# Spectral filter, soft MoE and GLU on one core: filters loaded by units instead of by channel halves, and the second step's first stage moved into a block

## The chip, the cores and the metric

The kernel runs on one core of a Trainium2 chip. The metric is the time of one execution in microseconds of device time; the median of three executions is taken.

## The reference

```python
# x (8, 3072, 256); filt_r, filt_i (1537, 256)
X = np.fft.rfft(x, axis=1)
Y = X * (filt_r + 1j * filt_i)[None]
y = np.fft.irfft(Y, n=3072, axis=1)          # (8, 3072, 256)
x = y.reshape(8 * 3072, 256)
logits = x @ phi                              # 32 slots, 4 for each of 8 experts
d = softmax(logits, axis=0); c = softmax(logits, axis=1)
slot = d.T @ x                                # (32, 256), then each expert: relu(slot @ w1) @ w2
x = c @ slot_out
g = x @ w_gate
out = (g * sigmoid(g) * (x @ w_val)) @ w_out
```

## The kernel before

The Fourier transform of each of the 8 sequences is a product of three small ones. A **step** is one sequence and one half of its 256 channels, so there are 16 steps. The tile `x` of a step, 96 partitions of 2x16x128 numbers (1.573 MB), comes by four transfers in runs of 512 bytes (`load_x`, two for each `k`).

For a step, `s1_chunk` is done four times, for 32 channels each: 8 matmuls in two passes from `x` into the PSUM tile `s1`, of which there is one place, a VectorE transpose into `sg`, and a ScalarE copy into `b` (`spread`). Then come six **units**, each with `s2_unit`: 16 matmuls (`X`, two PSUM places) from `b` and the constants `fwd`, two VectorE products `P` and `Q` with the filters in the tile `ft`, and a difference and a sum on GpSimd into `y`. Unit `u` uses rows `2u` and `2u+1` of `ft` (128x12x2x256 numbers, 3.146 MB) and columns `4u` to `4u+3` of `fwd` (1.573 MB). `tr_unit` (tile `T`) and `phi_pair` (tile `L`) of a unit follow two and four units later.

Each engine runs its instructions in the order in which the program writes them. The main loop goes through the 96 units in that order, and after unit `u` of a step it writes chunk `u-1` of the next step's first stage (`plan`), so that chunks lie between units. The end corrections of `load_filters` (`memset` and two multiplications by 0.5 of row 0 on GpSimd) stand in GpSimd's order ahead of all `y`. They are written once for each half of the channels, since `load_filters(h)` loads one half: in runs of 512 bytes.

Beside this, from unit 4 on, the generator `conv` is advanced twice for each unit (`aside`). It loads pieces of the GLU weights as 64-bit words into one of two places `raw` (262 KB each), and converts each in four parts: two VectorE operations (tiles `ex` and `mn`), three on ScalarE, one on VectorE (`ex`), two on GpSimd, then a store to `wgd` and the load of the next piece but one. VectorE's first such operation is written behind unit 4 and ahead of `P` of unit 5; the one for the third piece is written behind unit 8 and ahead of `P` of unit 9.

Nearly all transfers are issued by SyncE in program order, and each waits for the eighth one before it. `inv` (1.573 MB of constants) is read first by the chain that follows the first sequence, in the third step. The order of the loads at the start is

```python
csm, x of step 0 (4), fwd, load_filters(0), phi, x of step 1 (4),
load_filters(1), inv,          # then from the loop:
x of step 2 (4), raw (2), half of x of step 3 (2), ...
```

After the 96 units come the experts (some 385 to 480 us) and then the GLU, which takes the rest.

Of the kernel before, what the change touches and what calls it, by code (L numbers as in the profile page):

```python
# [7 lines left out]
F32 = mybir.dt.float32  # L8
# [9 lines left out]
NB, SEQ, D, E = 8, 3072, 256, 32  # L18
# [61 lines left out]
def spectral_softmoe_glu_kernel(  # L80
# [17 lines left out]
    nc = tc.nc  # L98
    pe, dve, act, pool = nc.tensor, nc.vector, nc.scalar, nc.gpsimd
# [32 lines left out]
    def phase1():  # L132
        with ExitStack() as c1:
# [11 lines left out]
            ps_s1 = c1.enter_context(tc.tile_pool(name="ps_s1", bufs=1, space=PSUM))  # L145
# [3 lines left out]
            ps_c = c1.enter_context(tc.tile_pool(name="ps_c", bufs=1, space=PSUM))  # L149

            ft = big.tile([128, 12, 2, D], F32, name="ft")
            inv = big.tile([128, NJ, 128], F32, name="inv")
            fwd = big.tile([128, NJ, 128], F32, name="fwd")
            nyq = big.tile([1, D], F32, name="nyq")
# [9 lines left out]
            def load_x(step, k):  # L164
                b, h = divmod(step, 2)
                if b >= NB:
                    return

                if k == 0:
                    xt[step] = xp[step % 2].tile([128, 2, 16, 128], F32, tag="x", name="x")  # L170
                xr = x[b].rearrange("(p h r n) d -> r h p n d", h=2, r=2, n=16)
                for r in range(2):
                    nc.sync.dma_start(  # L173
                        out=xt[step][64 * r:64 * r + 48, k], in_=xr[r, k, :, :, h * 128:(h + 1) * 128]
                    )

            def load_filters(h):
                hs, o, n = slice(h * 128, (h + 1) * 128), h * 128, 128
                for ri, fl in enumerate((filt_r, filt_i)):
                    for par in range(2):  # L180
                        nc.sync.dma_start(
                            out=ft[par * 64:par * 64 + 32, :, ri, hs],
                            in_=bass.AP(fl.tensor, par * D + o, [[48 * D, 32], [2 * D, 12], [1, n]]),
                        )
                        k = 1 - par
                        nc.sync.dma_start(
                            out=ft[par * 64 + 32:par * 64 + 64, k:, ri, hs],
                            in_=bass.AP(
                                fl.tensor,
                                (48 - par - 2 * k) * D + o,  # L190
                                [[48 * D, 32], [-2 * D, 12 - k], [1, n]],
                            ),
                        )
                    nc.sync.dma_start(
                        out=ft[32:64, 0, ri, hs],
                        in_=bass.AP(fl.tensor, 24 * D + o, [[48 * D, 32], [1, n]]),
                    )
                nc.sync.dma_start(out=nyq[:, hs], in_=filt_r[SEQ // 2:SEQ // 2 + 1, hs])
                pool.memset(ft[0:1, 0, 1, hs], 0.0)
                pool.tensor_scalar_mul(ft[0:1, 0, 0, hs], ft[0:1, 0, 0, hs], 0.5)  # L200
                pool.tensor_scalar_mul(nyq[:, hs], nyq[:, hs], 0.5)

            def s1_chunk(step, c):
                if step >= 2 * NB:
                    return
                if c == 0:
                    bt[step] = bp[step % 2].tile([128, NJ, 128], F32, tag="b", name="b")
                ps = ps_s1.tile([128, 32, 32], F32, tag="s1", name="s1")
                for r in range(2):
                    for k in range(2):  # L210
                        pe.matmul(  # L211
                            out=ps[64 * k:64 * k + 64, 16 * r:16 * r + 16, :],
                            lhsT=s1t_sb[64 * r:64 * r + 48, :],
                            rhs=xt[step][64 * r:64 * r + 48, k, :, c * 32:(c + 1) * 32],
                            tile_position=(64 * r, 64 * k),
                        )

                sg = sgp.tile([128, 16, 32, 2], F32, tag="sg", name="sg")
                dve.transpose(out=sg.rearrange("p j d k -> p d j k"), in_=ps.rearrange("p n d -> p d n"))  # L219
                staged.append((step, c, sg))  # L220
                if c == 3:
                    xt.pop(step)

            def spread():

                while staged:
                    step, c, sg = staged.pop(0)
                    act.copy(  # L228
                        bt[step][:, :, c * 32:(c + 1) * 32].rearrange("p (j k) d -> p j k d", k=2),
                        sg[:, 0:NJ // 2].rearrange("p j d k -> p j k d"),  # L230
                    )

            def s2_unit(step, u):
                b, h = divmod(step, 2)
                bb = bt[step]
                ps = ps_x.tile([128, 2, 2, 128], F32, tag="X", name="X")
                for i in range(2):
                    pp = 2 * u + i
                    for ri in range(2):
                        for par in range(2):  # L240
                            j = 2 * pp + par
                            pe.matmul(  # L242
                                out=ps[par * 64:(par + 1) * 64, i, ri, :],
                                lhsT=fwd[:, j, ri * 64:(ri + 1) * 64],
                                rhs=bb[:, j, :],
                            )
                f = ft[:, 2 * u:2 * u + 2, :, h * 128:(h + 1) * 128]
                P = pq.tile([128, 2, 2, 128], F32, tag="P", name="P", bufs=3)
                Q = pq.tile([128, 2, 2, 128], F32, tag="P", name="Q", bufs=3)
                dve.tensor_tensor(out=P, in0=ps, in1=f, op=ALU.mult)  # L250
                dve.tensor_tensor(out=Q, in0=ps, in1=f[:, :, ::-1, :], op=ALU.mult)  # L251
                if u == 0:
                    dve.tensor_tensor(
                        out=Q[0:1, 0, 1, :],
                        in0=ps[0:1, 0, 1, :],
                        in1=nyq[:, h * 128:(h + 1) * 128],
                        op=ALU.mult,
                    )
                k = (6 * b + u - 6 * NB) % NY
                if h == 0:  # L260
                    yt[b, u] = yp[(k >= 2) + (k >= NY - 6)].tile([128, 2, 2, D], F32, tag=f"y{k}", name="y")
                y = yt[b, u][:, :, :, h * 128:(h + 1) * 128]
                pool.tensor_tensor(out=y[:, :, 0, :], in0=P[:, :, 0, :], in1=P[:, :, 1, :], op=ALU.subtract)  # L263
                eng = dve if (step, u) == (2 * NB - 1, 5) else pool
                eng.tensor_tensor(out=y[:, :, 1, :], in0=Q[:, :, 0, :], in1=Q[:, :, 1, :], op=ALU.add)
# [343 lines left out]
            nc.sync.dma_start(out=csm, in_=c_small)  # L609
            load_x(0, 0)  # L610
            load_x(0, 1)
            nc.sync.dma_start(out=fwd, in_=c_fwd)
            load_filters(0)
            nc.sync.dma_start(out=phi_sb, in_=phi.rearrange("(t p) e -> p t e", p=128))
            load_x(1, 0)
            load_x(1, 1)
            load_filters(1)
            nc.sync.dma_start(out=inv, in_=c_inv)
            dve.memset(ones, 1.0)
            dve.memset(expo, -916.0 * (1 << 23))  # L620
            side = [conv(), first_weights()]
# [7 lines left out]
            plan = [[], [0], [1], [2], [3], []]  # L629
# [18 lines left out]
            def tail_ops(i):  # L648
                if 0 <= i - 2 < len(units):
                    tr_unit(*units[i - 2])  # L650
                if i - 4 >= 0 and i % 2 == 0 and i - 3 < len(units):
                    s, u = units[i - 4]
                    phi_pair(s, u // 2)
                    if s % 2 == 1 and u == 4:
                        ready.append((s // 2, chain(s // 2, s // 2 == NB - 1)))
# [5 lines left out]
            for i, (s, u) in enumerate(units):  # L661
                if u in (0, 2):
                    load_x(s + 2, u // 2)
                s2_unit(s, u)
                tail_ops(i)
                spread()
                if i >= 4:
                    aside()
                on = pump(1)
                for c in plan[u]:  # L670
                    s1_chunk(s + 1, c)
                if u == 5:
                    bt.pop(s)
                if on or i >= len(units) - 10:
                    pump(1)
                if i == 88:
                    kept(0)
                    kept(1)
                if i >= 4:
                    aside()  # L680
# [349 lines left out]
```

## Time and profile before

| | |
|---|---|
| median of 3 runs | 1562.45 us (1561.62 to 1564.56) |
| profiled execution | 1558.03 us, its span 1556.2 us |
| TensorE, VectorE, ScalarE, GpSimd busy | 1477.5, 1182.4, 954.1, 238.3 us |
| mean granted TensorE clock | 0.985 of full speed |

The span goes from the first to the last instruction of the profiled execution. The busy times are unions over the whole span, and say nothing of a stage by themselves; the change touches the first 80 us or so. Names such as `X<-b,fwd` are the program's tiles, result first. In rows, PE is TensorE, DVE VectorE, ACT ScalarE, POOL GpSimd and SP SyncE.

### The profile page before, as it was taken

Reading aid. Unit: us, or ns where it says so; the run is one execution under the profiler, and the core shown is the slowest. Engines: PE = TensorE matmul, PEld = TensorE weight load, DVE = VectorE, ACT = ScalarE, POOL = GpSimd, SP = SyncE. Lnnn points to the kernel's source line nnn. Section 1 sums busy time; section 2 is a strip of 40 time slices with the busy share of each in tenths; the row PEclk is TensorE's granted clock in tenths of the full one; section 3 lists DMA queues with packets and bytes.
Section 4 is the critical chain, followed back from the end, with each engine's and each line's share of the span. In section 5 each row is a group of like instructions: output and inputs, shape, how many; then the busy total and the mean of one; then the engine's idle time right before and its main releaser. Section 6 shows DMA issues by size and latency. Waiting matters only on the chain.

```text
span 1556.2 us, 26502 instructions
## 1 busy us (share of the span) xinstructions
PE 1477.5 (95%) x10218; PEld 1146.6 (74%) x10218; DVE 1182.4 (76%) x1960; ACT 954.1 (61%) x1808; POOL 238.3 (15%) x300
## 2 busy tenths in 40 slices
PE   4799999999778999999999999999999999999998
PEld 1355555555436888888888888888888888888887
DVE  1597887877528887887797788789788878877775
ACT  1365655644316766766776676677667667666665
POOL 0465555553201000000000010000000000000000
PEclk9799999988999999999999999999999999999999
DMA  9997787782592021112102111211211211120111
GB/s 174 181 163 123 131 138 135 128 120 95 206 319 82 14 68 38 28 42 51 28 19 63 38 28 42 51 28 33 50 38 28 62 31 28 35 61 15 27 28 27
DMA packets 105297, 116.58 MB, mean 75 GB/s; under 512 B 14770, under 2 KB 85172, under 8 KB 104916
## 3 DMA queue, kind: packets, MB, share of 16 engines
q1 hardware_dynamic: 102260, 110.44, 33.8%
q10 hardware_dynamic: 2656, 3.93, 0.9%
q8 instruction: 80, 1.31, 0.4%
q0 software_dynamic: 256, 0.52, 0.1%
q14 instruction: 45, 0.37, 0.1%
HBM read 68.21 MB, written 34.60 MB: 66 GB/s over the span
## 4 chain that ended last, share of the span: by engine, by line
PE 84%; DVE 4%; DMA 4%; SPq 3%; ACT 2%; issue 2%; POOL 0%; ACTq 0%; DVEq 0%; POOLq 0%
PE o L944 34%; PE o L948 17%; PE V L917 9%; PE G L916 9%; PE X L242 4%; PE T L273 3%; PE s L211 2%; DMA c<-cd 1%; PE c L455 1%; SPq L173 1%; SPq L129 1%; PE L L282 1%; PE c L417 1%; DMA raw<-in_moe_w_gate_dram 1%; DVE sg L219 1%
## 5 line engine op out<-in xcount | busy, mean ns | idle before, releaser
L944 PE MATMUL o<-wo,hi 128*128 128x512 f32 x2304 | 832.5, 396 | 0.0
L948 PE MATMUL o<-wo,lo 128*128 128x256 f32 x2304 | 646.6, 281 | 0.2 <-DVE lo L933 0.2
L919 ACT ACTIVATE s<-G 128x512 f32<-128x512 f32 x576 | 344.6, 598 | 320.5 <-PE G L916 317.2
L925 DVE TENSOR_TENSOR h<-V,s 128x512 f32<-128x512 f32 x576 | 394.9, 686 | 171.3 <-ACT s L919 168.8
L944 PEld LDWEIGHTS o<-wo,hi 128*128 128x128 f32 x2304 | 433.4, 188 | 102.9
L948 PEld LDWEIGHTS o<-wo,lo 128*128 128x128 f32 x2304 | 435.2, 189 | 25.4 <-DVE lo L933 0.6
L933 DVE TENSOR_TENSOR lo<-h,hi 128x512 fp32r<-128x512 f32 x576 | 417.0, 724 | 0.1
L932 ACT CAST hi<-h 128x512 fp32r<-128x512 f32 x576 | 354.4, 615 | 14.4 <-DVE h L925 10.2
L916 PE MATMUL G<-c,g 128*128 128x512 f32 x576 | 228.4, 397 | 2.2 <-DMA g<-gl 1.6
L917 PE MATMUL V<-c,v 128*128 128x512 f32 x576 | 227.8, 396 | 2.2 <-DVE h L925 1.7
L242 PEld LDWEIGHTS X<-b,fwd 128*64 128x64 f32 x1536 | 86.9, 143 | 76.7 <-issue 51.7
L275 ACT COPY yt<-T 128x512 f32<-128x512 f32 x96 | 55.9, 583 | 136.3 <-PE T L273 132.8
L916 PEld LDWEIGHTS G<-c,g 128*128 128x128 f32 x576 | 108.5, 188 | 28.2 <-issue 3.4
L219 DVE STREAM_TRANSPOSE sg<-s 128x1024 f32<-128x1024 f32 x64 | 79.4, 1240 | 57.2 <-PE s L211 57.0
L242 PE MATMUL X<-b,fwd 128*64 128x128 f32 x1536 | 110.4, 289 | 11.8 <-ACT b L228 10.3
L917 PEld LDWEIGHTS V<-c,v 128*128 128x128 f32 x576 | 109.0, 189 | 4.0 <-DVE h L925 2.8
L863 POOL TENSOR_TENSOR lg<-lg,mx 96x1024 f32<-96x1024 f32 x7 | 16.8, 2397 | 585.4 <-DVE mx L861 585.4
L211 PE MATMUL s<-x,csm 48*64 48x512 f32 x512 | 84.7, 679 | 22.0 <-DMA x<-in_x_dram 15.2
L958 DVE TENSOR_TENSOR ot<-o,tmp 128x256 f32<-128x256 f32 x192 | 70.1, 423 | 38.4 <-ACT tmp L957 38.4
L263 POOL TENSOR_TENSOR y<-P 128x256 f32<-128x256 f32 x96 | 70.2, 732 | 144.7 <-DVE P L250 144.3
L251 DVE TENSOR_TENSOR Q<-X,ft 128x512 f32<-128x512 f32 x96 | 64.9, 677 | 13.7 <-POOL y L263 13.7
L228 ACT COPY b<-sg 128x768 f32<-128x768 f32 x64 | 58.6, 916 | 26.6 <-DVE sg L219 26.3
(194 smaller groups left out, 1021.1 us busy)
## 6 DMA issues: line engine op xcount, KB each, us to landing
x<-in_x_dram SPq DMA_DIRECT2D x64, 384.0 KB, 8.1
out_dram<-ot SPq DMA_DIRECT2D x192, 128.0 KB, 2.2
w<-in_moe_w_dram SPq DMA_DIRECT2D x16, 1024.0 KB, 9.6
c<-ch SPq DMA_DIRECT2D x42, 128.0 KB, 2.4
c<-cl SPq DMA_DIRECT2D x42, 128.0 KB, 2.4
raw<-in_moe_w_gate_dram SPq DMA_DIRECT2D x12, 256.0 KB, 4.5
lgd<-lg ACTq DMA_DIRECT2D x16, 192.0 KB, 4.4
raw<-in_moe_w_val_dram SPq DMA_DIRECT2D x12, 256.0 KB, 3.5
```

The lines of the kernel that those rows point to most:

```text
L211: pe.matmul(out=ps[64 * k:64 * k + 64, 16 * r:16 * r + 16, :], lhsT=s1t_sb[64 * r:64 * r + 48, :], rhs=xt[step][64 * r:64 * r + 48, k, :, ...
L219: dve.transpose(out=sg.rearrange("p j d k -> p d j k"), in_=ps.rearrange("p n d -> p d n"))
L242: pe.matmul(out=ps[par * 64:(par + 1) * 64, i, ri, :], lhsT=fwd[:, j, ri * 64:(ri + 1) * 64], rhs=bb[:, j, :],)
L263: pool.tensor_tensor(out=y[:, :, 0, :], in0=P[:, :, 0, :], in1=P[:, :, 1, :], op=ALU.subtract)
L916: pe.matmul(out=pg, lhsT=g4[c][:, fs], rhs=c4[b][:, q, G, :])
L917: pe.matmul(out=pv, lhsT=v4[c][:, fs], rhs=c4[b][:, q, G, :])
L919: act.activation(s, pg, AF.Silu)
L925: dve.tensor_tensor(out=h, in0=pv, in1=s, op=ALU.mult)
L932: act.copy(hi, h)
L933: dve.tensor_tensor(out=lo, in0=h, in1=hi, op=ALU.subtract)
L944: pe.matmul(out=a, lhsT=hi[:, ts], rhs=wo[f].rearrange("p k d -> p (k d)"), start=(f == 0), stop=(f == NF - 1), skip_group_check=True,)
L948: pe.matmul(out=a[:, D:2 * D], lhsT=lo[:, ts], rhs=wo[f][:, 0, :], start=False, stop=(f == NF - 1), skip_group_check=True,)
```

## The change

`load_filters` takes a group of six rows of `ft` (three units) with all 256 channels, in runs of 1 KB; the end corrections are written once, with the first group. `fwd` is loaded in two halves, each ahead of the group that needs it. Two of the four transfers of step 0's `x` are issued by ScalarE. The order at the start is now

```python
csm, x of step 0 (2; the other 2 by ScalarE), first half of fwd, load_filters(0),
second half of fwd, load_filters(1), phi, x of step 1 (4),   # then from the loop:
x of step 2 (4), raw (2), half of x of step 3 (2), inv, ...
```

The four chunks of step 1 are all written behind unit 5 of step 0, instead of one each behind units 1 to 4, and in the first two steps odd chunks take the PSUM place of the tile `c`, which the chains use later.

```diff
-                    nc.sync.dma_start(
+                    (nc.scalar if r and not step else nc.sync).dma_start(
...
-            def load_filters(h):
-                hs, o, n = slice(h * 128, (h + 1) * 128), h * 128, 128
+            def load_filters(g):
+                lo, hi = 6 * g, 6 * g + 6
...
-                            out=ft[par * 64:par * 64 + 32, :, ri, hs],
-                            in_=bass.AP(fl.tensor, par * D + o, [[48 * D, 32], [2 * D, 12], [1, n]]),
+                            out=ft[par * 64:par * 64 + 32, lo:hi, ri, :],
+                            in_=bass.AP(fl.tensor, (par + 2 * lo) * D, [[48 * D, 32], [2 * D, 6], [1, D]]),
...
+                if g == 0:
+                    nc.sync.dma_start(out=nyq, in_=filt_r[SEQ // 2:SEQ // 2 + 1, :])
+                    pool.memset(ft[0:1, 0, 1, :], 0.0)
+                    pool.tensor_scalar_mul(ft[0:1, 0, 0, :], ft[0:1, 0, 0, :], 0.5)
+                    pool.tensor_scalar_mul(nyq, nyq, 0.5)
...
-                ps = ps_s1.tile([128, 32, 32], F32, tag="s1", name="s1")
+                if step < 2 and c % 2:
+                    ps = ps_c.tile([128, 1024], F32, tag="c", name="s1").rearrange("p (n d) -> p n d", d=32)
+                else:
+                    ps = ps_s1.tile([128, 32, 32], F32, tag="s1", name="s1")
...
-            nc.sync.dma_start(out=fwd, in_=c_fwd)
+            nc.sync.dma_start(out=fwd[:, 0:12], in_=c_fwd[:, 0:12])
             load_filters(0)
+            nc.sync.dma_start(out=fwd[:, 12:24], in_=c_fwd[:, 12:24])
+            load_filters(1)
...
-            load_filters(1)
-            nc.sync.dma_start(out=inv, in_=c_inv)
...
+                if i == 6:
+                    nc.sync.dma_start(out=inv, in_=c_inv)
                 s2_unit(s, u)
...
-                for c in plan[u]:
+                for c in plan[u] if i >= 6 else range(4) if i == 5 else ():
                     s1_chunk(s + 1, c)
+                    if i == 5:
+                        spread()
```

VectorE, units 4 and 5 of step 0 before: the transposes into `sg` are chunks of step 1, `raw` is the first piece of the weights, and each pair `P`, `Q` is one unit.

```order
L219 STREAM_TRANSPOSE sg<-s_318 128x32x16x2
L250 TENSOR_TENSOR P<-X,ft 128x512
L251 TENSOR_TENSOR Q<-X,ft 128x512
L219 STREAM_TRANSPOSE sg<-s_360 128x32x16x2
L558 TENSOR_SCALAR ex<-raw 128x256
L559 TENSOR_SCALAR mn<-raw 128x256
L250 TENSOR_TENSOR P<-X,ft 128x512
L251 TENSOR_TENSOR Q<-X,ft 128x512
L565 SCALAR_TENSOR_TENSOR ex<-raw,ex 128x256
L250 TENSOR_TENSOR P<-X,ft 128x512
L251 TENSOR_TENSOR Q<-X,ft 128x512
```

The same place on VectorE in the change (line numbers are five higher there).

```order
L255 TENSOR_TENSOR P<-X,ft 128x512
L256 TENSOR_TENSOR Q<-X,ft 128x512
L563 TENSOR_SCALAR ex<-raw 128x256
L564 TENSOR_SCALAR mn<-raw 128x256
L255 TENSOR_TENSOR P<-X,ft 128x512
L256 TENSOR_TENSOR Q<-X,ft 128x512
L224 STREAM_TRANSPOSE sg<-s_360 128x32x16x2
L224 STREAM_TRANSPOSE sg<-s_368 128x32x16x2
L224 STREAM_TRANSPOSE sg<-s_376 128x32x16x2
L224 STREAM_TRANSPOSE sg<-s_384 128x32x16x2
L570 SCALAR_TENSOR_TENSOR ex<-raw,ex 128x256
L255 TENSOR_TENSOR P<-X,ft 128x512
```

The four transposes of step 1 now stand behind the first operation on `raw` and ahead of unit 6 (the last row).

SyncE's issues in the change, from step 1's `x` on (one row for several alike).

```order
L621 DMA phi_sb<-in_moe_phi_dram 128x2x32
L173 DMA x<-in_x_dram 48x16x128 x8
L549 DMA raw<-in_moe_w_gate_dram 128x512 x2
L173 DMA x<-in_x_dram 48x16x128 x2
L670 DMA inv<-in_const_inv_dram 128x3072
L574 DMA wgd<-mn 128x256
L549 DMA raw<-in_moe_w_gate_dram 128x512
```

`inv` has moved from ahead of step 2's `x` to behind the first half of step 3's, and stands ahead of the third piece of `raw` (the last row).

## Rows read from the trace of the kernel before

**Rows 1.** The page's first line

```profile
span 1556.2 us, 26502 instructions
```

**Rows 2.** Chain of waits that ended last: start us, us, what

```profile
53.58 10.44 DMA raw<-in_moe_w_gate_dram
```

**Rows 3.** Timeline, VectorE: start us, us, what, in brackets idle before and releaser

```profile
28.88 1.25 DVE L219 STREAM_TRANSPOSE sg<-s 128x1024 f32<-128x1024 f32 x1 [2.18 <-PE s L211]
...
49.18 0.69 DVE L251 TENSOR_TENSOR Q<-X,ft 128x512 f32<-128x512 f32 x1 [13.73 <-POOL y L263]
...
64.05 0.29 DVE L558 TENSOR_SCALAR ex<-raw 128x256 int32<-128x256 int32 x1 [3.03 <-DMA raw<-in_moe_w_gate_dram]
...
65.66 0.57 DVE L565 SCALAR_TENSOR_TENSOR ex<-raw,ex 128x256 int32<-128x256 int32 x1
...
71.15 0.68 DVE L250 TENSOR_TENSOR P<-X,ft 128x512 f32<-128x512 f32 x1
...
74.95 0.29 DVE L558 TENSOR_SCALAR ex<-raw 128x256 int32<-128x256 int32 x1 [1.37 <-DMA raw<-in_moe_w_gate_dram]
```

**Rows 4.** Timeline, GpSimd, columns as in Rows 3

```profile
45.19 0.19 POOL L199 MEMSET ft<- 1x128 f32 x1 [15.91 <-DMA ft<-in_filt_i_dram]
...
48.43 0.71 POOL L263 TENSOR_TENSOR y<-P 128x256 f32<-128x256 f32 x1
```

**Rows 5.** Stretches, a header and its rows

```profile
core 0: us, PE busy (x) PEld busy (x) DVE busy (x) ACT busy (x) POOL busy (x), PEclk, DMA share, GB/s
5.00:12.50 7.50, 1.93 (x2) 0.29 (x2) 0.00 (x0) 0.00 (x0) 0.00 (x0) 1.00 1.25 128
20.00:27.50 7.50, 4.68 (x20) 0.88 (x24) 2.50 (x2) 2.48 (x3) 0.72 (x2) 1.00 1.24 189
30.00:37.50 7.50, 4.40 (x34) 3.34 (x34) 2.30 (x5) 0.88 (x1) 0.00 (x0) 1.00 1.25 149
47.50:50.00 2.50, 0.59 (x2) 0.30 (x3) 0.82 (x2) 0.00 (x0) 2.06 (x4) 0.50 0.96 388
...
432.50:445.00 12.50, 11.65 (x124) 4.66 (x120) 2.21 (x4) 2.48 (x5) 0.00 (x0) 1.00 1.09 348
```

**Rows 6.** Timeline, TensorE matmuls, columns as in Rows 3

```profile
19.97 1.98 PE L211 MATMUL s<-x,csm 48*64 48x512 f32 x8 [1.34 <-DVE sg L219]
...
31.10 3.40 PE L242 MATMUL X<-b,fwd 128*64 128x128 f32 x32 [2.35 <-ACT b L228]
...
49.88 0.90 PE L273 MATMUL T<-csm,y 128*128 128x128 f32 x3 [0.21 <-POOL y L265]
...
62.76 1.09 PE L242 MATMUL X<-b,fwd 128*64 128x128 f32 x16 [1.51 <-ACT b L228]
63.78 0.66 PE L273 MATMUL T<-csm,y 128*128 128x128 f32 x4
64.37 0.64 PE L282 MATMUL L<-yt,phi_sb 128*32 128x256 f32 x8
...
67.41 1.09 PE L211 MATMUL s<-x,csm 48*64 48x512 f32 x8
```

**Rows 7.** Timeline, ScalarE, columns as in Rows 3

```profile
30.17 0.88 ACT L228 COPY b<-sg 128x768 f32<-128x768 f32 x1 [2.55 <-DVE sg L219]
```

**Rows 8.** Stretches, columns as in Rows 5

```profile
43.80:49.20 5.40, 0.00 (x0) 0.00 (x1) 0.02 (x1) 0.00 (x0) 1.95 (x5) 0.50 1.16 281
49.20:54.50 5.30, 4.80 (x26) 2.49 (x28) 4.25 (x5) 1.39 (x2) 3.40 (x5) 0.50 1.12 225
54.60:62.00 7.40, 6.64 (x72) 3.54 (x68) 4.96 (x6) 3.80 (x7) 2.84 (x4) 1.00 1.23 151
```

**Rows 9.** The loads of raw, first 80 us

```profile
DMA to landing us min/median/max: 4.1/7.4/10.4
```

**Rows 10.** Stretch after the startup, columns as in Rows 5

```profile
80.00:280.00 200.00, 188.05 (x2310) 111.97 (x2314) 166.46 (x300) 118.30 (x246) 118.39 (x163) 1.00 0.78 136
```

**Rows 11.** The first reader of inv

```profile
L356 PE MATMUL c<-inv,lha x32: 272/273/273, 95.6 to 96.4; 128*32 128x128 f32 x32
```

More of the change, by code (lines that the diff above doesn't have):

```diff
@@ L181, in load_filters @@
                         nc.sync.dma_start(
-                            out=ft[par * 64:par * 64 + 32, :, ri, hs],
-                            in_=bass.AP(fl.tensor, par * D + o, [[48 * D, 32], [2 * D, 12], [1, n]]),
+                            out=ft[par * 64:par * 64 + 32, lo:hi, ri, :],
+                            in_=bass.AP(fl.tensor, (par + 2 * lo) * D, [[48 * D, 32], [2 * D, 6], [1, D]]),
                         )
-                        k = 1 - par
+                        k = max(lo, 1 - par)
                         nc.sync.dma_start(
-                            out=ft[par * 64 + 32:par * 64 + 64, k:, ri, hs],
+                            out=ft[par * 64 + 32:par * 64 + 64, k:hi, ri, :],
                             in_=bass.AP(
-                                fl.tensor,
-                                (48 - par - 2 * k) * D + o,
-                                [[48 * D, 32], [-2 * D, 12 - k], [1, n]],
-                            ),
-                        )
[L194 to L201, printed above, removed]
+                                fl.tensor, (48 - par - 2 * k) * D, [[48 * D, 32], [-2 * D, hi - k], [1, D]]
+                            ),
+                        )
+                    if g == 0:
+                        nc.sync.dma_start(
+                            out=ft[32:64, 0, ri, :],
+                            in_=bass.AP(fl.tensor, 24 * D, [[48 * D, 32], [1, D]]),
+                        )
+                if g == 0:
+                    nc.sync.dma_start(out=nyq, in_=filt_r[SEQ // 2:SEQ // 2 + 1, :])
+                    pool.memset(ft[0:1, 0, 1, :], 0.0)
+                    pool.tensor_scalar_mul(ft[0:1, 0, 0, :], ft[0:1, 0, 0, :], 0.5)
+                    pool.tensor_scalar_mul(nyq, nyq, 0.5)
             def s1_chunk(step, c):
```

## The prediction

> **What bounds the kernel now.** I read the chain of waits first, then the timelines of the engines that it names, then the transfers in stretches. All that the change touches lies in the first 80 us of a span of 1556.2 us [rows 1]. In the chain of waits the longest piece there is the wait for the first `raw`, from 53.58 on and 10.44 us long [rows 2]. The reader is to see that two waits follow each other on VectorE. It first stands 13.73 us in front of a `Q` at 49.18, because `y` on GpSimd has not freed a buffer [rows 3]: GpSimd stood 15.91 us in front of the second end correction, whose filters had not landed, and did its first `y` at 48.43, behind that [rows 4]. Then, after five units in haste, VectorE stands 3.03 us more in front of the first operation on `raw`, which starts at 64.05 [rows 3]. In all this time the transfers run without a pause (share 0.96 to 1.25 in the stretches up to 62 us [rows 5, 8]). So the startup ends when the stream of transfers reaches `raw`, and the compute of the first six units has had time to spare. Behind the startup TensorE is busy 188.05 of 200 us, the DMA engines 0.78 [rows 10]: compute sets the pace there, nothing can give back what the startup gained or lost, and I carry a shift seen at 75 us to the end. The place to read it is VectorE's operation on the third `raw`, at 74.95 after a wait of 1.37 us [rows 3], so VectorE itself was there at 73.58.
>
> **The stream up to the first `raw`.** Call T the start of VectorE's first operation on `raw`, 64.05 before. Ahead of that load stand the same bytes as before, but for three things.
> `inv` is gone from there: 1.573 MB, and the stretch in which it moves runs at 388 GB/s [rows 5], so 4.05 us.
> The filters, 3.146 MB, went in 512-byte runs at 189 GB/s [rows 5], 16.65 us. In runs of 1 KB the nearest rows are the expert loads of 1 KB rows at 432 to 445 us: 348 GB/s [rows 5], which makes 9.05 us and saves 7.6. The ends are 0 (the rate is that of bytes, and stays) and 8.3 (a run costs the same whatever its length, so half). I take 7.6, a measured rate of the same run length and direction.
> The Trainium skill (DMA: Bandwidth & Descriptors, Specifications) puts the least transfer for line rate at 512 bytes. By that the longer runs would save nothing and T would be 7.6 us later than I make it; the two rates just named disagree, and it stands below as the slower rival.
> Step 0's `x`, 1.573 MB, moved at 128 GB/s, 12.3 us; the same shape in step 1 moved at 149 [rows 5], 10.55 us. Now two queues bring it. No row shows two queues loading at once. The ends are 12.3 us as before, and 8.3 us at the filters' 189 GB/s. I take the row between, 10.55, and save 1.7.
> T becomes 64.05 - 4.05 - 7.6 - 1.7 = 50.7.
>
> **What the other edits are worth by themselves.** The end corrections once: GpSimd's stop up to 45.19 goes, and with it VectorE's 13.73 us. It brings nothing more than T, because what is late next is `raw`. Two PSUM places: the first chunks follow each other at 1.98 us of TensorE [rows 6] (the low clock, since the same chunk takes 1.09 later; the 1.00 of the early stretches is no more than a missing record) instead of one in about 3.35 (1.98 and the idle before it). This too is covered. Even if the units of step 0 began no earlier than the first `X` before, at 31.10, six of them at the low clock (`X` 3.40 / 2 = 1.70, `T` 0.90 x 4/3 = 1.2 [rows 6]) would be through at 48.5, ahead of T. Step 1's `x` lands some 13 us ahead of T (step 2's `x`, 10.55, and the rest behind it), so two chunks of the block are in PSUM when VectorE comes to them. Without that cover each late microsecond would count in full.
>
> **What the block costs.** Before, VectorE was free for unit 6 right behind `Q` of unit 5, T + 1.6 (64.05 to 65.66 [rows 3]), and step 1's chunks had been done in the waits. Now four transposes of 1.25 us [rows 3] stand there, and unit 6's `X` needs the last of the four copies. Two transposes end at T + 4.1. The third chunk can enter the first PSUM place at T + 2.85. TensorE has then had almost nothing to do for some 8 us. Before, a stretch of 5.4 us without matmuls left the granted clock at 0.50 (1.2 GHz), and 5.3 us of nearly unbroken work at 0.50 came before 1.00 (2.4 GHz) [rows 8]. So I cost the block at the low clock: chunks at T + 4.85 and T + 6.8 (1.98 each), transpose to T + 8.1, copy of 0.88 [rows 7] to T + 9.0, `X` of unit 6 to T + 10.7, then `T`, `L` (0.64 at the high clock, 1.1 taken) and `X` of unit 7 to T + 14.7. That is 5.7 us of work without a break, and I let the clock rise there. `T` 0.66 and the next chunk 1.09 [rows 6] end at T + 16.45, its transpose at T + 17.7, the operation of 0.57 on `ex` at T + 18.3. From there to the third `raw` it is as before 73.58 - 71.15 = 2.43 (from `P` of unit 8 [rows 3]): T + 20.7 = 71.4.
>
> **`inv` in its new place.** SyncE issues half of step 3's `x` when TensorE has done the block, T + 6.8 = 57.5; behind it come `inv`, a store and the third `raw`. 0.786 MB at 149 GB/s is 5.3, `inv` 4.05, and a `raw` by itself takes at least 4.1 us from issue to landing [rows 9], with the store in it: 70.95. That is just ahead of the 71.4 at which VectorE wants it, so the 1.37 us of waiting from before goes as well. The chain reads `inv` first at 95.6 [rows 11], when it has been there for 25 us.
>
> **Sum.** The third `raw` is begun at 71.4 instead of 74.95: 3.55 us earlier. The trace is of an execution of 1558.03 us (span 1556.2), 4.4 below the median of the three runs, which is 1562.45. I take the difference off both: 1558.9, and a profiled execution of about 1554.5.
>
> **Rivals.**
> *More is won.* Either the clock is up in the block (1.09 for a chunk, 7.5 to the last copy, T + 17.0 = 67.7; but then the third `raw`, at T + 5.2 + 13.45 = 69.35, is the later), or `x` over two queues moves like the filters (T = 48.4, 69.1). 5.6 and 5.85 us: 1556.6 to 1556.9. For it: the chunks of the block and the ones ahead of it might keep TensorE busy enough. Against it: the idle stretch in front.
> *Little or nothing.* Two queues don't help `x`: T = 52.4, third `raw` at 73.1, 1.85 us, 1560.6. If the clock also stays low through the next `T` and chunk (1.45 us more), 0.4 us are left: 1562.05. For it: share 1.25 at 128 GB/s [rows 5] says that the engines were taken, not that requests were missing. The Trainium skill says so too (DMA: Bandwidth & Descriptors, Issuing engines are not separate DMA queues): queues share the same engines, and a second issuer saves only issue time; no run here shows it.
> *Slower.* The filters' runs of 1 KB move no faster than those of 512 bytes, being strided in a way that the expert weights aren't. T = 50.7 + 7.6 = 58.3, and the block, which no longer hides in waits, puts the third `raw` at 79.0: 4.05 us later, 1566.5. It is even at T = 54.25, and slower by 3.1 us from T = 57.35 on, when the filters save less than 0.95 us (200 GB/s). Against it: 189 and 348 GB/s are both rates of loads from HBM with the engines full, and the packets are alike but for their length.
> *The change doesn't do what it says.* The waits go, but later stages absorb it: 1562.4. Against it stands TensorE's 94% behind the startup.
>
> **How the numbers follow.** 0.2% of the time is 3.1 us, about what a measurement of this kernel can tell from no change. The forecast (1557.8 to 1560.0) has 0.45, more won 0.17, little or nothing 0.26, slower 0.08, absorbed 0.04. Two thirds of the forecast lie below 1559.35, so faster has 0.31 + 0.17 = 0.48, same 0.14 + 0.26 + 0.04 = 0.44, slower 0.08. The range takes in the forecast, most of what is won more, and the case in which little is left: 1556.2 to 1562.8.
>
> **What the profile after would show.** The filters' stretch at about 350 GB/s; the first end correction by 25 us, the first `y` soon after and no stop of GpSimd behind it; VectorE idle in front of the first `raw` for more than 5 us, and that begun at 49 to 52.5; third and fourth chunk of step 1 at some 1.98 us each; unit 6's `P` at T + 10.8; the third `raw` begun at about 71.4, with a wait under 1 us. The prediction is wrong if T is past 54, if unit 6 starts sooner than 8.6 us after T, or if the third `raw` waits for `inv` by more than 1.5 us.

## The result, and the profile after

The change makes the kernel slower: 1570.70 us in the median of four runs (1570.24 to 1573.44) against 1563.43 for the kernel before (1561.62 to 1564.56), a ratio of 1.0051 with a 95% interval of 1.0037 to 1.0065, so 7 to 8 us. 1558.9 us had been predicted, 3.55 us less than the kernel before.

The profiled execution took 1570.73 us. The page's first line:

```profile
span 1568.6 us, 26500 instructions
```

Against [rows 1] that is 12.4 us more, but only part of it belongs to the change. `P` of unit 12 starts 7.2 us later than before (90.76 against 83.53), that of unit 95, the last, 7.75 us later (412.43 against 404.68): the shift arises at the start and is carried nearly unchanged. The 4.6 us behind unit 95 I take for a difference between executions, since another execution of the kernel before (below) shows 5.1 us there too.

The timeline of VectorE after, columns as in [rows 3], whose rows it answers (line numbers are five higher):

```profile
25.02 0.69 DVE L255 TENSOR_TENSOR P<-X,ft 128x512 f32<-128x512 f32 x1 [2.17 <-PE X L247]
...
35.11 0.69 DVE L255 TENSOR_TENSOR P<-X,ft 128x512 f32<-128x512 f32 x1 [5.78 <-DMA phi_sb<-in_moe_phi_dram]
...
59.80 0.29 DVE L563 TENSOR_SCALAR ex<-raw 128x256 int32<-128x256 int32 x1 [22.20 <-DMA raw<-in_moe_w_gate_dram]
...
61.41 2.37 DVE L224 STREAM_TRANSPOSE sg<-s 128x1024 f32<-128x1024 f32 x2
64.83 1.25 DVE L224 STREAM_TRANSPOSE sg<-s 128x1024 f32<-128x1024 f32 x1 [1.05 <-PE s L216]
66.54 1.25 DVE L224 STREAM_TRANSPOSE sg<-s 128x1024 f32<-128x1024 f32 x1 [0.46 <-PE s L216]
...
70.85 0.69 DVE L255 TENSOR_TENSOR P<-X,ft 128x512 f32<-128x512 f32 x1 [2.76 <-PE X L247]
...
77.48 0.68 DVE L255 TENSOR_TENSOR P<-X,ft 128x512 f32<-128x512 f32 x1
...
82.41 0.29 DVE L563 TENSOR_SCALAR ex<-raw 128x256 int32<-128x256 int32 x1 [2.10 <-DMA raw<-in_moe_w_gate_dram]
...
90.76 0.69 DVE L255 TENSOR_TENSOR P<-X,ft 128x512 f32<-128x512 f32 x1 [0.36 <-PE X L247]
```

Two rows of before that go with them, `P` of units 6 and 12:

```profile
66.15 0.68 DVE L250 TENSOR_TENSOR P<-X,ft 128x512 f32<-128x512 f32 x1
...
83.53 0.68 DVE L250 TENSOR_TENSOR P<-X,ft 128x512 f32<-128x512 f32 x1
```

The reader is to see one long wait of 22.20 us where [rows 3] has two (13.73 and 3.03). The 5.78 us ahead of it, in front of unit 3, is the wait for the second group of filters (the chain of waits below). Unit 0 starts at 25.02, five units are through by 37.6, and then VectorE stands in front of the first `raw` with the four transposes of step 1 queued behind that operation. `raw` is there at 59.80, 4.25 us sooner than before. But `P` of unit 6 starts 11.05 us behind it (70.85), before 2.1 us (66.15), and the third `raw` comes at 82.41 instead of 74.95.

GpSimd after, which answers to [rows 4]:

```profile
22.20 0.30 POOL L200 MEMSET ft<- 1x256 f32 x1 [21.76 <-DMA ft<-in_filt_i_dram]
...
25.80 0.72 POOL L268 TENSOR_TENSOR y<-P 128x256 f32<-128x256 f32 x1 [0.20 <-DVE P L255]
```

The end corrections are done early and the first `y` follows at 25.80 instead of 48.43. This part of the change does what it says and brings nothing by itself, as the prediction had it.

The chain of waits after, columns as in [rows 2]; "SPq" is SyncE's queue, standing until one of the eight transfers in flight has landed:

```profile
26.94 7.90 DMA ft<-in_filt_i_dram
...
40.16 2.78 SPq L173
42.99 2.81 SPq L173
45.84 2.78 SPq L173
48.66 11.11 DMA raw<-in_moe_w_gate_dram
...
61.49 1.17 DVE sg L224
62.70 3.74 PE s L216 x16
66.54 1.26 DVE sg L224
67.82 0.90 ACT b L233
68.76 2.00 PE X L247 x16
70.85 0.70 DVE P L255
...
75.51 6.88 DMA raw<-in_moe_w_gate_dram
```

Up to 59.8 the chain is the stream of transfers, then for 11 us it is the block: two transposes, two chunks, transpose, copy, `X` of unit 6, one behind the other. Then it is a transfer again, the third `raw`, for 6.88 us. Its load is issued no sooner than 75.51 because GpSimd does the last part of the first piece behind `y` of unit 6 (71.62), which stood behind the block.

Stretches after, columns as in [rows 5]:

```profile
5.00:12.50 7.50, 1.40 (x2) 0.28 (x2) 0.00 (x0) 0.00 (x0) 0.00 (x0) 1.00 1.26 149
17.50:20.00 2.50, 2.37 (x14) 0.27 (x8) 2.10 (x2) 0.89 (x1) 0.00 (x0) 1.00 1.15 204
27.50:32.50 5.00, 4.24 (x52) 3.15 (x48) 1.68 (x3) 1.76 (x3) 2.75 (x5) 1.00 1.14 208
40.00:55.00 15.00, 6.32 (x16) 1.05 (x14) 0.00 (x0) 0.16 (x1) 0.00 (x0) 0.59 1.26 137
42.80:73.50 30.70, 14.07 (x66) 5.08 (x68) 8.76 (x14) 5.64 (x9) 3.10 (x5) 0.50 0.88 111
80.00:280.00 200.00, 185.56 (x2253) 109.91 (x2252) 164.36 (x299) 116.15 (x242) 117.39 (x160) 1.00 0.78 136
```

The first row is step 0's `x`, 149 GB/s where it had 128 before [rows 5]. The second and third row are the filters: 204 and 208 GB/s, where 350 had been expected and 512-byte runs gave 189 [rows 5]. The fourth is `x` of steps 1 and 2: 137 GB/s, step 1's before 149. The fifth has the granted clock at 0.50 (1.2 GHz) through the wait and the whole block. The last is close to [rows 10]: TensorE busy 185.56 us against 188.05, share and rate of the transfers as before.

TensorE's matmuls at the block, which answer to [rows 6]:

```profile
62.70 3.69 PE L216 MATMUL s<-x,csm 48*64 48x512 f32 x16 [10.91 <-DVE sg L224]
...
68.76 1.98 PE L247 MATMUL X<-b,fwd 128*64 128x128 f32 x16 [2.36 <-ACT b L233]
...
72.72 1.46 PE L247 MATMUL X<-b,fwd 128*64 128x128 f32 x16
```

Third and fourth chunk (3.69 us together) and `X` of unit 6 (1.98) run at the low clock; it rises at 73.5, in `X` of unit 7.

### The profile page after: what moved, and what is told of

Same layout as the page of the kernel before. It is cut to its first block, busy times and chain, and to the rows that moved or that the text cites. A ratio compares the mean times of both kernels' runs of the same rounds, so it can differ in the third digit from the quotient of the medians.

```text
span 1568.6 us, 26500 instructions
## 1 busy us (share of the span) xinstructions
PE 1472.8 (94%) x10218; PEld 1145.7 (73%) x10218; DVE 1182.2 (75%) x1960; ACT 956.3 (61%) x1808; POOL 238.5 (15%) x297
## 4 chain that ended last, share of the span: by engine, by line
PE 83%; DMA 6%; DVE 4%; ACT 2%; SPq 2%; issue 2%; POOL 0%; ACTq 0%; DVEq 0%; POOLq 0%
PE o L954 34%; PE o L958 17%; PE G L926 9%; PE V L927 8%; PE X L247 4%; PE T L278 2%; PE s L216 2%; DMA c<-cd 1%; DMA raw<-in_moe_w_gate_dram 1%; PE c L460 1%; PE L L287 1%; SPq L129 1%; PE c L422 1%; DMA ft<-in_filt_r_dram 1%; ACT b L233 1%
## 5 line engine op out<-in xcount | busy, mean ns | idle before, releaser
L216 PE MATMUL s<-x,csm 48*64 48x512 f32 x512 | 80.3, 667 | 32.9 <-DMA x<-in_x_dram 18.9
L255 DVE TENSOR_TENSOR P<-X,ft 128x512 f32<-128x512 f32 x96 | 65.1, 679 | 17.4 <-PE X L247 9.9
L270 POOL TENSOR_TENSOR y<-Q 128x256 f32<-128x256 f32 x95 | 73.1, 770 | 2.8 <-DVE Q L258 2.8
```

Source lines behind the costliest of these rows:

```text
L216: pe.matmul(out=ps[64 * k:64 * k + 64, 16 * r:16 * r + 16, :], lhsT=s1t_sb[64 * r:64 * r + 48, :], rhs=xt[step][64 * r:64 * r + 48, k, :, ...
```

## The experiments

T is again the start of VectorE's first operation on `raw`. Starts in the profiled executions, in us; in e3, e4, e9 and e10 conversions begin later, so that T no longer bounds unit 6 and the third `raw` belongs to a later unit:

| kernel | T | `P`, unit 6 | third `raw` | `P`, unit 12 | ratio to before (95%) |
|---|---|---|---|---|---|
| before | 64.05 | 66.15 | 74.95 | 83.53 | |
| before, again | 67.34 | 69.45 | 78.18 | 86.71 | |
| after | 59.80 | 70.85 | 82.41 | 90.76 | 1.0051 (1.0037 to 1.0065) |
| e1 chunks between units | 58.55 | 61.59 | 70.98 | 79.70 | 0.9991 (0.9975 to 1.0006) |
| e2 block alone | 61.75 | 72.79 | 81.86 | 90.80 | 1.0059 (1.0039 to 1.0080) |
| e3 conversion 1 unit later | 60.01 | 58.48 | 72.26 | 76.70 | 0.9982 (0.9969 to 0.9996) |
| e4 conversion 2 units later | 59.46 | 57.93 | 76.94 | 79.05 | 0.9937 (0.9917 to 0.9957) |
| e5 `raw` ahead of `x` | 47.59 | 58.63 | 71.17 | 81.43 | 0.9983 (0.9969 to 0.9997) |
| e6 filters, contiguous source | 57.61 | 68.65 | 78.81 | 87.17 | |
| e7 filters, 128 partitions | 49.64 | 60.68 | 70.84 | 79.52 | |
| e8 `x` by one queue | 58.10 | 69.15 | 79.57 | 87.92 | |
| e9 e4, filters by two queues | 60.56 | 58.76 | 77.81 | 79.92 | 0.9923 (0.9904 to 0.9942) |
| e10 before, conversion later | 68.19 | 66.66 | 80.61 | 83.72 | 0.9964 (0.9951 to 0.9977) |
| e11 `inv` back | 63.62 | 74.67 | 84.48 | 93.42 | |

e6, e7, e8 and e11 have one execution each: 1568.22, 1557.62, 1569.15 and 1571.80 us, beside some 1565 us of the kernel before.

My theory was that the block, standing on VectorE behind the first operation on `raw`, costs time where the chunks between the units had cost none, and that T had not come down far enough to pay for it. The rivals: the block costs wherever it stands; the loads of the change are what is slow.

**e1: the chunks between the units again**, all the rest as after.

```diff
-                for c in plan[u] if i >= 6 else range(4) if i == 5 else ():
+                for c in plan[u]:
                     s1_chunk(s + 1, c)
-                    if i == 5:
-                        spread()
```

> The change with one part undone: step 1's chunks stand between units 1 to 4 again, all new loads stay. Theory: the block is what costs; it stands on VectorE behind the first operation on raw and no longer hides in the wait for it. Then the first raw is begun at about 59.8 as in the change, P of unit 6 follows 2.1 us later as in the kernel before (near 62, 66.15 there), and the whole is 3 to 4.5 us faster than the kernel before (ratio 0.997 to 0.998). Rival: the loads cost (inv ahead of the third raw, slower x), the block only shifts work; then this stays slower than the kernel before by 3 us or more.

VectorE in e1:

```profile
58.55 0.25 DVE L563 TENSOR_SCALAR ex<-raw 128x256 int32<-128x256 int32 x1
...
61.59 0.69 DVE L255 TENSOR_TENSOR P<-X,ft 128x512 f32<-128x512 f32 x1 [0.21 <-PE X L247]
```

The slowdown is gone: unit 6 follows the first `raw` by 3 us, and unit 12 is 3.8 us ahead of before. But the time is 0.9991, no change, where 0.997 to 0.998 had been expected: of the 3.8 us, 1.8 are left at unit 95 (402.84 against 404.68).

**e2: the kernel before with the block and the two PSUM places, and no other part of the change.**

```diff
-                ps = ps_s1.tile([128, 32, 32], F32, tag="s1", name="s1")
+                if step < 2 and c % 2:
+                    ps = ps_c.tile([128, 1024], F32, tag="c", name="s1").rearrange("p (n d) -> p n d", d=32)
+                else:
+                    ps = ps_s1.tile([128, 32, 32], F32, tag="s1", name="s1")
...
-                for c in plan[u]:
+                for c in plan[u] if i >= 6 else range(4) if i == 5 else ():
                     s1_chunk(s + 1, c)
+                    if i == 5:
+                        spread()
```

> The kernel before with one part of the change alone: the block of step 1's chunks behind unit 5 and the two PSUM places; loads and end corrections as before. Theory: the first raw is begun at 64.05 as before, P of unit 6 follows about 11 us later instead of 2.1, and the whole is 8 to 11 us slower (ratio 1.005 to 1.007). Rival (the loads cost): within 2 us of the kernel before.

The block alone gives the whole slowdown, 1.0059, with unit 6 at T + 11.04. The two runs add up: 1.0059 with the block alone and 0.9991 with all but the block make 1.0050, and 1.0051 is what both together took. VectorE in e2:

```profile
61.75 0.29 DVE L561 TENSOR_SCALAR ex<-raw 128x256 int32<-128x256 int32 x1 [7.81 <-DMA raw<-in_moe_w_gate_dram]
...
72.79 0.69 DVE L253 TENSOR_TENSOR P<-X,ft 128x512 f32<-128x512 f32 x1 [2.75 <-issue]
```

**e3: the conversion's work from unit 6 on**, its first loads where they were, so that the block stands ahead of the wait for `raw`.

```diff
-                if i >= 4:
+                if i == 4 or i >= 6:
                     aside()
...
-                if i >= 4:
+                if i >= 6:
                     aside()
```

> The change, but the conversion's work on raw begins at unit 6 instead of unit 4 (its two loads are still issued at unit 4), so that on VectorE the block stands ahead of the first operation on raw. Theory: the block then runs in the wait for raw; its chunks begin when step 1's x has landed (near 47), P of unit 6 comes at 56 to 59 instead of 70.85, the first raw at about 59.8 behind it, and unit 9 is 5 to 8 us earlier than in the kernel before; the whole 4 to 8 us faster (ratio 0.995 to 0.9975). Rival: the block costs its 9 us wherever it stands (low clock, last copy ahead of unit 6); then this is no faster than the kernel before.

VectorE in e3:

```profile
49.04 1.25 DVE L224 STREAM_TRANSPOSE sg<-s 128x1024 f32<-128x1024 f32 x1 [10.89 <-PE s L216]
...
58.48 0.69 DVE L255 TENSOR_TENSOR P<-X,ft 128x512 f32<-128x512 f32 x1 [3.05 <-PE X L247]
...
60.01 0.27 DVE L563 TENSOR_SCALAR ex<-raw 128x256 int32<-128x256 int32 x1
```

The same four transposes at the same low clock (granted 0.50 from 47 to 58.5 us) now run while `raw` is still on its way, and cost nothing: unit 6 starts ahead of the first `raw`, unit 12 is 6.8 us ahead of before. 1.8 us of this are left at unit 95, and 0.9982 is measured. "The block costs wherever it stands" falls.

**The kernel before, profiled again.**

> The kernel before, unchanged, profiled once more beside the others. If step 1's and step 2's x move at 149 to 153 GB/s again, the 137 GB/s of the changed kernel comes from the change; if they move at about 137, from the chip. The GLU stage's end should lie nearer to the median than in the first profile, which was 4.4 us below it.

1568.34 us; T is 3.3 us later than in the first profile of the same kernel. Step 1's `x` took 2.92 us per transfer, 2.5 in the first. So T varies by some us from execution to execution, and a single profile's T says no more than that. The same holds for the shifts: against this profile of before the changed kernel is 4.2 us later at the third `raw`, not 7.5, and 2.5 us later at unit 95 (412.43 against 409.92), not 7.75.

**e4: the conversion two units later.**

```diff
-                if i >= 4:
+                if i == 4 or i >= 7:
                     aside()
...
-                if i >= 4:
+                if i >= 6:
                     aside()
```

> As e3, but the conversion is put off by two whole units (its two loads at unit 4, its work from the second half of unit 6 on), so that from there each of its pieces stands at the same place between chunks as in the kernel before; in e3 it had moved by one and a half units, and a lead of 7 us at unit 12 had shrunk to 2 at unit 72. Theory: the lead of e3 comes from the block standing ahead of raw, the shrinking from the other place between the chunks. Then the lead at unit 12 is 5 to 8 us again and at unit 72 still over 4, and the ratio is 0.9945 to 0.9975. Rival: the lead melts away whatever the place, since the pace behind the startup has slack; then it is at 2 us by unit 72 and the ratio near 0.998.

0.9937, faster than both kernels (1554.92 us against 1564.73). VectorE in e4:

```profile
57.93 0.69 DVE L255 TENSOR_TENSOR P<-X,ft 128x512 f32<-128x512 f32 x1 [3.06 <-PE X L247]
...
76.94 0.29 DVE L563 TENSOR_SCALAR ex<-raw 128x256 int32<-128x256 int32 x1 [3.69 <-DMA raw<-in_moe_w_gate_dram]
```

The lead over before is 4.5 us at unit 12, 4.15 at unit 72, 9.2 at unit 84: half of the gain arises far behind the startup, which I had not expected. e10 takes it apart.

**e5: the first two `raw` ahead of step 2's `x`**, the order on VectorE as after.

```diff
             side = [conv(), first_weights()]
+            next(side[0])
...
-                if i >= 4:
+                if i >= 5:
                     aside()
                 on = pump(1)
```

> The changed kernel with the first two loads of raw issued ahead of step 2's x; the order of VectorE is untouched, so the block still stands behind the first operation on raw. Theory: only the time at which raw lands matters. The first raw is begun at 48 to 50 instead of 59.8, right behind step 1's x, P of unit 6 follows about 11 us behind it (59 to 61), the third raw is begun at 70 to 72, and the whole is 2 to 5 us faster than the kernel before (ratio 0.997 to 0.999). Rival (the block costs wherever raw lands): slower than the kernel before, ratio above 1.003.

VectorE in e5:

```profile
47.59 0.29 DVE L563 TENSOR_SCALAR ex<-raw 128x256 int32<-128x256 int32 x1 [10.64 <-DMA raw<-in_moe_w_gate_dram]
...
58.63 0.69 DVE L255 TENSOR_TENSOR P<-X,ft 128x512 f32<-128x512 f32 x1 [2.75 <-PE X L247]
...
71.17 0.30 DVE L563 TENSOR_SCALAR ex<-raw 128x256 int32<-128x256 int32 x1 [2.84 <-DMA raw<-in_moe_w_gate_dram]
```

The block is as long as after (T + 11.04) and stands behind the same wait; only T is 12.2 us earlier, and the slowdown is gone (0.9983). So what the block costs in the end hangs on when T is.

**e6: the filters' source contiguous**, target and runs as after.

```diff
-in_=bass.AP(fl.tensor, (par + 2 * lo) * D, [[48 * D, 32], [2 * D, 6], [1, D]]),
+in_=bass.AP(fl.tensor, (4 * g + 2 * par) * 192 * D, [[6 * D, 32], [D, 6], [1, D]]),
...
-fl.tensor, (48 - par - 2 * k) * D, [[48 * D, 32], [-2 * D, hi - k], [1, D]]
+fl.tensor, (4 * g + 2 * par + 1) * 192 * D, [[6 * D, 32], [D, hi - k], [1, D]]
```

> The changed kernel, its filters read from contiguous blocks of 192 or 160 rows instead of every second row 48 rows apart (so with other filters than the reference's); the same 32 partitions are written in the same runs of 1 KB. If the stride in HBM holds the filters at 205 to 210 GB/s, they move near the 348 GB/s of the expert weights now, a load of 192 KB in about 0.56 us; if the 32 partitions of the target do, they stay near 207 GB/s, 0.95 us.

A stretch of e6 in which only filters move:

```profile
27.50:30.00 2.50, 2.50 (x32) 1.87 (x28) 1.70 (x3) 0.58 (x1) 2.50 (x4) 1.00 1.15 207
```

The same rate. That the source is strided was the prediction's reason for its slower rival; it is not the cause.

**e7: rows of the same length and stride, but into all 128 partitions.**

```diff
-                            out=ft[par * 64:par * 64 + 32, lo:hi, ri, :],
-                            in_=bass.AP(fl.tensor, (par + 2 * lo) * D, [[48 * D, 32], [2 * D, 6], [1, D]]),
+                            out=ft[:, lo + 2 * q:lo + 2 * q + 2, ri, :],
+                            in_=bass.AP(x.tensor, (6 * g + 2 * q + ri) * 2 * D, [[48 * D, 128], [2 * D, 2], [1, D]]),
```

> The changed kernel, its filters replaced by rows of x with the same stride of 48 rows between partitions and the same runs of 1 KB, but each transfer writes two rows of all 128 partitions instead of six of 32 (so with other filters than the reference's, and without the small transfers for row 0). If the target's 32 partitions hold the rate, it goes to about 348 GB/s; if the stride in HBM does, it stays near 207 GB/s.

Two stretches of e7, its first and second group of filters, then VectorE:

```profile
15.00:17.50 2.50, 2.50 (x14) 0.55 (x10) 0.64 (x1) 0.00 (x0) 0.00 (x0) 1.00 1.04 348
22.50:25.00 2.50, 1.57 (x16) 1.57 (x18) 0.00 (x0) 0.88 (x1) 0.00 (x0) 0.60 1.09 349
```

```profile
49.64 0.29 DVE L551 TENSOR_SCALAR ex<-raw 128x256 int32<-128x256 int32 x1 [16.61 <-DMA raw<-in_moe_w_gate_dram]
...
60.68 0.69 DVE L243 TENSOR_TENSOR P<-X,ft 128x512 f32<-128x512 f32 x1 [2.76 <-PE X L235]
...
70.84 0.62 DVE L551 TENSOR_SCALAR ex<-raw 128x256 int32<-128x256 int32 x1 [0.41 <-DMA raw<-in_moe_w_gate_dram]
```

348 GB/s, the rate of the expert loads [rows 5]. So the number of partitions that a transfer writes held the filters' rate, not the length of the runs or their place in HBM. e7 also writes two rows into each partition at a time instead of six, but the expert loads write eight and have the same rate. With it T is 49.64 and the third `raw` 70.84, where the prediction had 50.7 and 71.4, and its one execution took 1557.62 us, below the fastest of 17 of the kernel before (1560.12): with the filters at the predicted rate the change goes the predicted way, as far as one execution tells.

**e8: step 0's `x` by SyncE alone.**

```diff
-                    (nc.scalar if r and not step else nc.sync).dma_start(
+                    nc.sync.dma_start(
```

> The changed kernel with step 0's x issued by SyncE alone again. If the two queues moved it faster, as the first landing of its last transfer suggests (13.5 to 14.6 us in the kernels with two queues, 15.3 and 15.8 in the two profiles of the kernel before), it lands at 15.3 to 16 again and the first product P starts 1 to 2 us later than 25.0. If they share the engines and gain nothing, both stay where they are in the changed kernel.

The last of the four transfers of step 0's `x` begins to land at 14.04 us, after at 14.61, and T is 58.10, within what executions differ by. Only unit 0 starts later (26.64 instead of 25.02). In this pair the second queue brought the stream nothing. Over all executions it is less plain: with one queue (before twice, e2, e8, e10) that landing begins at 13.8 to 15.8 us, 14.9 in the mean, with two (after, e1, e3 to e7, e11) at 13.2 to 14.6, 13.7 in the mean. Whether the second queue is worth about 1 us is thus neither shown nor ruled out.

**e9: e4, and half of the filters by GpSimd's queue.**

```diff
-                        nc.sync.dma_start(
+                        (nc.gpsimd if par else nc.sync).dma_start(
```

> e4 with the filters of every second row (those that go to partitions 64 to 127) issued by GpSimd, so that two queues write two sets of 32 partitions at once. If a transfer into 32 partitions is held by its target and not by the engines, the rate while both run goes from 207 to over 300 GB/s, step 1's x lands 3 to 5 us earlier than in e4, and the ratio falls to 0.990 to 0.993. Rival: the engines are taken (share 1.15 at 207 GB/s); then the rate stays and the ratio is that of e4, 0.9937.

0.9923, not to be told from e4's 0.9937. The two halves never ran at once: GpSimd's moved beside `x`, at 10 to 15 and 35 to 39.5 us, SyncE's alone, 206 GB/s from 20 to 23 us. Whether two transfers into 32 partitions each would move faster side by side stays open.

**e10: the kernel before with e4's edit to the conversion alone.**

```diff
-                if i >= 4:
+                if i == 4 or i >= 7:
                     aside()
...
-                if i >= 4:
+                if i >= 6:
                     aside()
```

> The kernel before with e4's edit alone: the conversion put off by two units, its two loads still issued at unit 4; loads, end corrections and chunks as before. It tells how much of e4's 9.8 us is the change's. Theory: at the start it saves at most the 3.03 us for which VectorE waits for the first raw, and what e4 gained between units 72 and 84 (5 us in the one profile, against the kernel before) comes with the later end of the conversion and stands here too: ratio 0.995 to 0.998. Rival: the gain there is chance or comes with the changed loads; then 0.998 to 1.000.

0.9964. Nothing is ahead at the start (`P` of unit 12 at 83.72 against 83.53, of unit 72 at 310.13 against 309.22), but at unit 84 it is 361.64 against 365.62. So e4's second half comes with the later conversion alone, and has nothing to do with the change; 0.9937 / 0.9964 = 0.997, some 4 us, is what the change's other parts are worth once the block no longer stands behind `raw`, though the two intervals together leave it between nothing and 8. What in units 72 to 84 gains from the later conversion I have not tested.

**e11: `inv` back ahead of step 2's `x`.**

```diff
             load_x(1, 1)
+            nc.sync.dma_start(out=inv, in_=c_inv)
...
-                if i == 6:
-                    nc.sync.dma_start(out=inv, in_=c_inv)
```

> The kernel after, with inv loaded where it was before, between step 1's x and step 2's x. Step 2's x moved in 2.45 to 2.6 us per 384 KB in the three kernels that load inv ahead of it, in 2.73 to 2.9 in those that don't. If the transfer ahead of it sets that rate, step 2's x takes 2.45 to 2.65 us per load here, and the first raw operation, later by inv's 4.05 and earlier by about 1.1, starts at about 62.8. If the rate only varies from run to run or comes from something else in the change, it stays at 2.7 to 2.9 and the first raw operation starts at about 63.9. In both cases P of unit 6 follows 11.0 us behind it, the third raw piece is wanted 20.5 us behind it and no longer waits (83.3 to 84.4), so that moving inv back costs 0.9 to 2.0 us at that point against the kernel after (82.41): what inv's move was worth there.

VectorE in e11:

```profile
63.62 0.30 DVE L563 TENSOR_SCALAR ex<-raw 128x256 int32<-128x256 int32 x1 [25.64 <-DMA raw<-in_moe_w_gate_dram]
...
84.48 0.29 DVE L563 TENSOR_SCALAR ex<-raw 128x256 int32<-128x256 int32 x1
```

T is 3.82 later, and the wait in front of the third `raw` is gone, so that moving `inv` was worth 2.07 us there, half of its 4.05, in this one pair of executions, while T alone differs by more between executions of one kernel. Step 2's `x` took 2.77 us per transfer, 2.84 after and 2.57 in the kernel before: `inv` ahead of it is not what sets that rate.

## Why the prediction was wrong

**The step that failed is the filters' price.** The prediction took 348 GB/s for runs of 1 KB from the expert loads and let T fall by 7.6 us for it. Measured are 204 to 208 GB/s: by the times at which each load begins to land, the filters took 15.5 us, before 17.1, and 1.6 us were saved. The nearest row agreed in the length of the run and the direction, but not in the partitions written: 128 against 32. e6 and e7 show that this decides. The Trainium skill has the rule that the prediction should have weighed (SBUF — State Buffer, Door 1: The DMA port swizzle): a transfer's rate goes by how many of 16 ports its partitions reach, 32 partitions reach 8 of them, about 218 GB/s. The trace agrees, with 208; it is no more than a ceiling here, since `x`, into 48 partitions in runs of 512 bytes, moved at 126 to 170 GB/s (5 to 12.5 us of before's second execution and of e1). The page that the prediction did weigh (DMA: Bandwidth & Descriptors, Specifications), by which 512-byte runs already have line rate, gave the better forecast here: longer runs brought 189 to 208 GB/s and no more, while runs of 1 KB into 128 partitions reached 348.

**T**, 59.80 instead of 50.7, 9.1 us late. By the same times: filters 6.0 less won than predicted; `x` of steps 1 and 2 took 22.9 us, before 20.4, so 2.5 lost that had no place in the sum; step 0's `x` won 0.7 instead of 1.7; `inv` 4.0, as predicted; small pieces some 0.5 the other way. What slowed `x` is open. It varies by itself (step 1's 10.1 and 11.7 us in the two profiles of before), but step 2's took 10.2 to 10.4 us in the four runs with before's order of loads (before twice, e2, e10), 11.4 after, 10.8 to 11.6 in e1, e3 to e6, e8 and e11, and 9.9 in e7. So about 1 us of it goes with the change's filter loads, and it goes away where these write 128 partitions; why is not shown.

**The block** was sized right: unit 6's `P` at T + 11.05 (T + 10.8 predicted), unit 8's at T + 17.7 (18.3), the third `raw` wanted at T + 20.5 (20.7), the clock low in it. e2, e5, e7 and e11 all have T + 11.04 or 11.05. From the first `raw` to the wanted third it is 20.5 us against 9.5 before: 11.0 more, against 4.25 saved ahead of it.

**`inv` in its new place** was to make no wait. The third `raw` waits 2.10 us, 0.73 more than before. Step 3's `x` and `inv` are issued when TensorE has done the block, from T + 6.7 on (T + 6.8 predicted), but that `x` landed 7.1 us later where 5.3 had been taken, and so `inv` was still moving when `raw` was issued at 75.51. e11 shows the wait go when `inv` does.

**The sum** of what was measured: -4.25 + 11.0 + 0.7 = 7.45 us, which is the shift at the third `raw` (82.41 against 74.95) and nearly that at the last unit (7.75). It is taken against the first profile of before. Against the second the shift at the third `raw` is 4.2 us, so that the sum meets the 7.3 us between the medians is in part luck; what the runs show without regard to the pair is the block's cost (e2) and that it is gone without the block (e1).

**The rivals.** "Slower" happened, with its own mechanism (filters hardly faster; it had T = 58.3 and the third `raw` at 79.0, 3.4 us less than measured, for T's 1.5 and the wait of 2.1 that it lacked); it was given 0.08 because the two rates were taken for rates of the same kind. Its reason, the stride, was wrong (e6). "Little or nothing" had two queues that don't help `x`, with the rule of the Trainium skill for it, by which a second issuer saves only issue time (DMA: Bandwidth & Descriptors, Issuing engines are not separate DMA queues): e8 agrees, but all executions together leave about 1 us open. "More is won" falls with T, and with the clock, which stayed at 0.50 in the block. "Absorbed" falls: the shift is carried to the end. But that nothing behind the startup can give back a shift holds for the change and not in general: e3's lead of 6.8 us at unit 12 was 1.8 at unit 95, with the conversion at another place.

## What to carry to other kernels

A transfer's price is looked up by the number of partitions that it writes as well as by its run length and direction; where the nearest row differs in one of them, the range has to reach to the row that shares it. Work that runs in the shadow of a wait is free only while the in-order queue has it ahead of the waiting instruction: moved behind it, the same four transposes cost 11 us, and moved ahead again (e3, e4) nothing. And when a block must stand behind a wait, ask first whether the load waited for can be issued sooner (e5).

## What the runs showed of the hardware that was not expected

Runs of 512 bytes into 32 partitions moved at 189 GB/s and runs of 1 KB at 204 to 208, these from strided and contiguous rows alike (after, e6); runs of 1 KB into 128 partitions moved at 348 (e7). Step 1's `x`, the same four transfers of 393 KB in 512-byte runs into 48 partitions, took 10.1 us in one execution of the kernel before and 11.7 in another.
